# Layer 2 of a three-part fp32 kernel: the activation behind the next unit's copy, seven units' activation in the second product, some sums on VectorE

## The chip, the cores and the metric

One core of one Trainium2 chip runs the whole kernel. The metric is device time in microseconds (us) of one execution; all engines work from their own instruction queues and wait for each other through semaphores. The engines are named as in the profile: PE (TensorE matmul), PEld (its weight load), DVE (VectorE), ACT (ScalarE), POOL (GpSimd) and SP (the queue that issues the DMAs).

## The reference

Windowed attention, then a first MLP, then a second one. Only the second MLP is touched:

```python
x = attention(q, k, v)                      # 4 x 8 heads x 576 x 64, window 64, then (2304, 512)
x = leaky(x @ w_in, 0.01) @ w_out           # 512 -> 2048 -> 512
h = x @ w_in2                               # (2304, 2048)
g = np.maximum(h, 0.0) + np.log1p(np.exp(-np.abs(h)))
out = g @ w_out2                            # (2304, 512)
```

## The kernel before

All products are fp32. Each fp32 operand is held as a high and a low part (`split`: a cast on ACT, then a subtract on DVE or POOL), and one fp32 product is three matmuls (`three`). In the second MLP ("layer 2") the products are also blocked 2 x 2 by a seven-product scheme: the operands get sums of their quarters (`winograd`), seven products are made (`ORDER`), and `combine` puts them together.

**First product of layer 2.** It is 24 units. A unit n is a pair p of blocks of the hidden dimension (eight pairs) times a chunk c of 768 tokens (three chunks), listed in `order`. `products(n, p, c)` makes it: seven products of six matmuls 128x384, each in a PSUM bank of its own. The eight banks go round, so a product can start only when the bank of the product eight places earlier has been read: the third product of a unit (index 2) waits for `u2` of the unit before, for example. `combine` reads the banks: first a copy q1 on ACT (L707), then eight adds on DVE (L706) that write the tile h in two halves; the tiles `h_xh` and `h_xl` take turns. Then for each half: DVE sets the sign bit of a copy, which makes -|h| (L698, an integer OR), ACT makes softplus of it (L699) and the relu of h (L700), POOL adds the two (L701), and SP stores the sum into DRAM at `hd[p]` (L702). The copies of -|h| lie in five places that the program calls `act_places` (two in `cv`, three in `kept64`; from unit 17 on only three).

**Second product of layer 2.** It is 40 steps (`steps2`): four chunks of 512 tokens and one of 256, times eight pairs. A step is 42 matmuls 128x256 (L792, L799, L800). What the steps need is made ahead by `advance(i)`: the four sums of step i+3 (`sums`, L255 on DVE), the splits of step i+2 (`spread`, three casts L759 on ACT, three subtracts L760 on DVE), and the load of step i+5 from `hd` into one of four tiles `in` (`load_h`). After the eighth step of a chunk `put_out` combines the banks (eight adds 128x512 on DVE).

**Order of the work.** The order on each engine is that of the program text, moved by `later` and `ordered`, which merge the queues of one unit or step with those beside it. `todo[n]` lists what is put beside unit n: the splits of the input chunk c=2 (`split_x2`, units 1 and 2), the loads of weights (`load_first`, `load_second`) and their splits (`split_pair`, L236 cast on ACT and L237 subtract), and from unit 17 on the preparation of the second product's first three steps (`advance(-3)` to `advance(-1)`). Weights of the second product are split with POOL's subtracts, those of the first with DVE's.

Of the kernel before, what the change touches and what calls it, by code (L numbers as in the profile page):

```python
# [14 lines left out]
AF = mybir.ActivationFunctionType  # L15
ALU = mybir.AluOpType
# [4 lines left out]
def tile_window_attention_two_mlps(  # L21
# [138 lines left out]
    cv = sb.tile([P, 3, DM], F32, tag="cv", bufs=1, name="cv")  # L160
# [31 lines left out]
    def take_rows(i, p, rows):  # L192
        W["pair", i, p] = {o: (row[:, 0], row[:, 1]) for row, o in zip(rows, USED)}

    def load_row(i, p, row, o):
        if split_too(i, p):
            nc.sync.dma_start(row.bitcast(F32), wd[i][p][:, o].rearrange("p a h x -> p a (h x)"))
        else:
            nc.sync.dma_start(row[:, 1].bitcast(F32), wd[i][p][:, o].rearrange("p h x -> p (h x)"))

    pair_tiles = {}

# [7 lines left out]

    def split_pair(i, p):
        for t in pair_tiles.pop((i, p)):
            split(t[:, :, 0], t[:, :, 1], t[:, :, 1].bitcast(F32), nc.gpsimd if i == 1 else None)

    def load_first(p):
        tags = ENDS if p == NF // 2 - 1 else ODD if p % 2 else EVEN
# [18 lines left out]
    def split(hi, lo, a, eng=None):  # L235
        i = nc.scalar.copy(hi, a)  # L236
        j = (eng or nc.vector).tensor_tensor(lo, a, hi.bitcast(F32), ALU.subtract)  # L237
        return i.ins, j.ins

    def winograd(t, b, plus, eng=None):  # L240

        if plus:
            todo = (
                (0, b[1][0], b[1][1], ALU.add), (2, b[0][0], b[1][0], ALU.subtract),
                (1, t[0], b[0][0], ALU.subtract), (3, b[0][1], t[1], ALU.subtract),
            )
        else:
            todo = (  # L250
                (0, b[0][1], b[0][0], ALU.subtract), (2, b[1][1], b[0][1], ALU.subtract),
                (1, b[1][1], t[0], ALU.subtract), (3, b[1][0], t[1], ALU.subtract),
            )
        for n, x, y, op in todo:
            (eng or nc.vector).tensor_tensor(t[n], x, y, op)  # L255

    kept = {}
# [292 lines left out]
    def x_tile(tag, name, shape, dt):  # L550
        return sb.tile(shape, dt, tag=tag, bufs=2, name=name)
# [20 lines left out]
    def split_x2(c, kk):  # L572
        x, ts = stage["x"], stage["t"]
        b = [[x[:, i, h * TH : (h + 1) * TH] for h in range(2)] for i in range(2)]
        if kk == 0:
            XB[c] = [
                wide(f"xb_{c}_{n}").rearrange("p a b -> p (a b)").rearrange("p (h k x) -> p h k x", h=2, k=2)
                for n in range(7)
            ]
        winograd([ts[:, n] for n in range(4)], b, False, nc.gpsimd)  # L580
        for d, a in zip(XB[c], (b[0][0], b[1][0], b[1][1])):
            split(d[:, 0, kk], d[:, 1, kk], a)

# [89 lines left out]
    def products(n, p, c):  # L673

        if "h" not in stage:
            stage["h"] = turns([x_tile(nm, f"h_{nm}", [P, 2, 2 * TH], F32) for nm in ("xh", "xl")])
        w, x = W["pair", 0, p], XB[c]

        def product(a, b):
            ps = next_bank([P, TH], f"p_{n}_{a}")
            (wh, wl) = (t.rearrange("p (k f) -> p k f", k=2) for t in w[a])
            for kk in range(2):
                three(ps, wh[:, kk], wl[:, kk], x[b][:, 0, kk], x[b][:, 1, kk], kk == 0, kk == 1)
            return ps

        t = lambda nm: sb.tile([P, TH], F32, tag="tmp", bufs=4, name=f"{nm}_{n}")
        h = next(stage["h"])
        behind.append(  # L690
            combine(
                (product(*o) for o in ORDER), t("q1"), t("u2"), t("u3"), t("v"),
                ((h[:, 0, :TH], h[:, 0, TH:]), (h[:, 1, :TH], h[:, 1, TH:])),
            )
        )
        for a in range(2):
            g = next(act_places)
            nc.vector.tensor_scalar(g.bitcast(I32), h[:, a].bitcast(I32), -(2**31), None, ALU.bitwise_or)  # L698
            nc.scalar.activation(g, g, AF.Softplus)  # L699
            nc.scalar.activation(h[:, a], h[:, a], AF.Relu)  # L700
            nc.gpsimd.tensor_tensor(g, h[:, a], g, ALU.add)  # L701
            nc.sync.dma_start(hd[p][:, a, c * 2 * TH : (c + 1) * 2 * TH], g)  # L702

    def combine(made, q1, u2, u3, v, to):

# [16 lines left out]
    sets, A, HT, ready = {}, {}, {}, {}  # L722
# [5 lines left out]
    HS = 4  # L728
# [26 lines left out]
    def spread(i):  # L755
# [7 lines left out]
        for x in range(4):  # L763
            A[i][4 + x] = [t[:, x] for t in four]

    def advance(i):

        for f, n in ((sums, 3), (spread, 2), (load_h, 5)):
            if (HS if f is load_h else 0) <= i + n < len(steps2):
                f(i + n)  # L770

# [215 lines left out]
    for item in HEAD:  # L987
        n = len(item.rstrip("0123456789"))
# [76 lines left out]
    N = len(order)  # L1065
# [4 lines left out]
    for p in range(2, NPR):  # L1070
        n = last_of[p - 2] if p < NPR - 1 else 8
        todo[n] += [(load_first, p)]
        todo[n + 2] += [(split_pair, 0, p)]

    def act_place():
        two = [kept["cv"][:, n * 2 * TH : (n + 1) * 2 * TH] for n in range(2)]
        more = [t.bitcast(F32)[:, : 2 * TH] for t in kept["64"]]
        for n in range(2 * (N - 7)):
            yield (two + more)[n % 5]
        while True:  # L1080
            yield from two + more[:1]

    act_places = act_place()
    chunks = [(t0, min(TO, NT - t0)) for t0 in range(0, NT, TO)]
    steps2 = [(k, t0, n, p) for k, (t0, n) in enumerate(chunks) for p in range(NPR)]

# [94 lines left out]
```

## Time and profile before

| | |
|---|---|
| median of three runs | 882.7 us (881.86 to 886.53) |
| the profiled execution, its own time | 881.52 us |
| its span, first to last instruction | 879.7 us |
| mean granted clock of TensorE | 0.992 |
| busy: PE, DVE, ACT, POOL | 844.1 (96%), 615.3 (70%), 462.2 (53%), 257.4 us (29%) |
| first matmul of layer 2, of its second product, end of the last | 492.7, 691.0, 875.6 us |

Times of single rows are of the profiled execution. Busy times of PE are of overlapping matmuls, so a full PE shows no gap but its matmuls start one "pitch" apart.

### The profile page before, as it was taken

What the parts mean: (1) busy time and instruction counts of PE and PEld (TensorE: products, weight loads), DVE (VectorE), ACT (ScalarE), POOL (GpSimd) and SP (SyncE); (2) the same over time, 40 slices, a digit from 0 to 9 for tenths busy, and PEclk for the clock granted to TensorE, in tenths of its full rate; (3) what the DMA queues carried; (4) which work ended last, traced back from release to release, by engine and by line L of the source; (5) the groups of instructions that cost most, each with busy time, mean ns of one, the idle gap of its engine ahead of it and who ended that gap; (6) DMA issues with size and microseconds to landing.
All of it is one profiled execution on the core that took longest, in us unless ns stands there. A gap on an engine that the chain in (4) does not pass through costs nothing. (4 is left out here: it accounts for less than half of the span.)

```text
span 879.7 us, 16530 instructions
## 1 busy us (share of the span) xinstructions
PE 844.1 (96%) x6072; PEld 822.1 (93%) x6072; DVE 615.3 (70%) x1104; ACT 462.2 (53%) x1037; POOL 257.4 (29%) x287
## 2 busy tenths in 40 slices
PE   7799999999999999999999999999987899999998
PEld 5789999899999999999999989988987899999998
DVE  5899743535436654344668788887899899887965
ACT  5888643545445444545556456635555453343432
POOL 3211000103423333233345365534556840000000
PEclk9999999999999999999999999999998999999999
DMA  9787667455958876565855345434455596443412
GB/s 206 195 218 228 189 150 134 110 113 148 249 149 235 221 208 181 157 174 165 251 171 159 105 144 174 150 120 143 162 193 173 186 327 213 121 144 98 144 53 92
DMA packets 213714, 148.56 MB, mean 169 GB/s; under 512 B 104832, under 2 KB 184064, under 8 KB 213632
## 3 DMA queue, kind: packets, MB, share of 16 engines
q1 hardware_dynamic: 213632, 147.49, 58.3%
q8 instruction: 48, 0.79, 0.4%
q14 instruction: 34, 0.28, 0.1%
HBM read 99.22 MB, written 54.53 MB: 175 GB/s over the span
## 5 line engine op out<-in xcount | busy, mean ns | idle before, releaser
L625 DVE TENSOR_TENSOR gl<-g,gh 128x384 fp32r<-128x384 f32 x96 | 59.9, 624 | 130.6 <-ACT gh L619 108.0
L593 PE MATMUL o<-gh,w 128*128 128x384 f32 x384 | 130.8, 341 | 0.4 <-DVE x L659 0.2
L593 PE MATMUL ph<-xh,w 128*128 128x384 f32 x384 | 130.5, 340 | 0.0
L594 PE MATMUL o<-gl,w 128*128 128x384 f32 x384 | 128.6, 335 | 0.6 <-DVE gl L625 0.5
L595 PE MATMUL ph<-xh,w 128*128 128x384 f32 x384 | 128.4, 334 | 0.0
L594 PE MATMUL ph<-xl,w 128*128 128x384 f32 x384 | 128.4, 334 | 0.0
L595 PE MATMUL o<-gh,w 128*128 128x384 f32 x360 | 120.6, 335 | 0.0
L613 ACT ACTIVATE g<-ph 128x384 f32<-128x384 f32 x96 | 46.9, 488 | 117.2 <-PE ph L595 117.0
L593 PEld LDWEIGHTS o<-gh,w 128*128 128x128 f32 x384 | 72.1, 188 | 3.0 <-issue 1.2
L593 PEld LDWEIGHTS ph<-xh,w 128*128 128x128 f32 x384 | 72.1, 188 | 1.2 <-issue 0.5
L594 PEld LDWEIGHTS o<-gl,w 128*128 128x128 f32 x384 | 72.1, 188 | 1.1 <-DVE gl L625 1.1
L594 PEld LDWEIGHTS ph<-xl,w 128*128 128x128 f32 x384 | 72.2, 188 | 0.0
L595 PEld LDWEIGHTS ph<-xh,w 128*128 128x128 f32 x384 | 72.1, 188 | 0.0
L792 PE MATMUL f<-wq,a 128*128 128x256 f32 x252 | 71.4, 283 | 0.0
L799 PE MATMUL f<-wq,a 128*128 128x256 f32 x252 | 71.3, 283 | 0.0
L800 PE MATMUL f<-wq,a 128*128 128x256 f32 x252 | 71.3, 283 | 0.0
L497 ACT ACTIVATE sm<-sm,nm 128x128 f32<-128x128 f32 x144 | 55.9, 391 | 26.2 <-DVE nm L486 26.1
L595 PEld LDWEIGHTS o<-gh,w 128*128 128x128 f32 x360 | 67.6, 188 | 0.3 <-issue 0.3
L510 POOL TENSOR_TENSOR sm<-sm,sums 128x512 f32<-128x512 f32 x36 | 38.6, 1072 | 87.7 <-DVE sums L506 54.3
L759 ACT CAST a<-in 128x512 fp32r<-128x512 f32 (+1 forms) x40 | 23.0, 576 | 56.7 <-issue 46.8
L760 DVE TENSOR_TENSOR a<-kept,a 128x1024 fp32r<-128x1024 f32 (+1 forms) x40 | 47.9, 1197 | 6.7 <-ACT a L759 6.7
L619 ACT CAST gh<-g 128x384 fp32r<-128x384 f32 x96 | 49.3, 514 | 2.4
(303 smaller groups left out, 2329.6 us busy)
## 6 DMA issues: line engine op xcount, KB each, us to landing
in<-hd SPq DMA_DIRECT2D x32, 512.0 KB, 4.6
hd<-cv SPq DMA_DIRECT2D x24, 384.0 KB, 2.6
hd<-kept SPq DMA_DIRECT2D x24, 384.0 KB, 2.5
wraw<-in_moe_w_out_dram SPq DMA_DIRECT2D x16, 512.0 KB, 4.5
wraw<-in_moe_w_in_dram SPq DMA_DIRECT2D x16, 512.0 KB, 4.1
kept<-in_moe_w_in_dram SPq DMA_DIRECT2D x16, 512.0 KB, 4.6
kept<-in_moe_w_out_dram SPq DMA_DIRECT2D x16, 512.0 KB, 4.0
wd<-kept_part SPq DMA_DIRECT2D x11, 512.0 KB, 4.3
```

The lines of the kernel that those rows point to most:

```text
L497: nc.scalar.activation(sm[:, p, :], sm[:, p, :], AF.Exp, bias=nm[:, p : p + 1], accum_out=sums[:, p : p + 1],)
L510: nc.gpsimd.tensor_tensor(sm, sm, sums.unsqueeze(2).to_broadcast([P, NP, P]), ALU.mult)
L593: nc.tensor.matmul(ps, wh, xh, start=start, stop=False)
L594: nc.tensor.matmul(ps, wh, xl, start=False, stop=False)
L595: nc.tensor.matmul(ps, wl, xh, start=False, stop=stop)
L613: nc.scalar.activation(g, ph, AF.Prelu, alpha=0.01)
L619: a = nc.scalar.copy(gh, g)
L625: b = nc.vector.tensor_tensor(gl, g, gh.bitcast(F32), ALU.subtract)
L760: last = [nc.vector.tensor_tensor(lo, a, hi.bitcast(F32), ALU.subtract) for (hi, lo), a in parts][-1].ins
L792: j = nc.tensor.matmul(ps, gh, wh, start=first and u == 0, stop=False, skip_group_check=True)
L799: nc.tensor.matmul(ps, gh, wl, start=False, stop=False, skip_group_check=True)
L800: j = nc.tensor.matmul(ps, gl, wh, start=False, stop=end, skip_group_check=True)
```

## The change

1. Unit n's softplus, relu, POOL add and store are put into a list and issued behind unit n+1's first copy q1 (`later(activate, lag=1)`); the OR stays with unit n.
2. For seven pairs (pair, chunk) in `RAW`, units 1, 17, 18, 20, 21, 22 and 23, no activation is made in the first product: h is stored as it is by one DMA (for the three of chunk 2 only its first 512 of 768 tokens; the last 256 go the old way, both halves in shapes 128x512). The second product makes it: `awake(i)`, called by `advance` four steps ahead, does OR on DVE, softplus on ACT, and max and add in one DVE instruction, in place in the tile `in`. That is ten of the 40 steps (6, 12, 13, 14, 20, 21, 22, 29, 30, 31), of which 12 and 13 for half of the tokens.
3. The pairs of the first product are made in the order `PAIRS` (the second product keeps its order).
4. `split_pair` of the second product's weights: pairs 0 to 2 subtract on DVE, not on POOL.
5. The sums of the input chunk c=2 (`winograd`, eight adds 128x384 in units 1 and 2) run on DVE, not on POOL.

```diff
+    PAIRS = (4, 3, 0, 1, 2, 5, 6, 7)
     def load_row(i, p, row, o):
+        d = wd[i][p if i else PAIRS[p]]
...
     def split_pair(i, p):
         for t in pair_tiles.pop((i, p)):
-            split(t[:, :, 0], t[:, :, 1], t[:, :, 1].bitcast(F32), nc.gpsimd if i == 1 else None)
+            split(t[:, :, 0], t[:, :, 1], t[:, :, 1].bitcast(F32), nc.gpsimd if i == 1 and p > 2 else None)
...
-        winograd([ts[:, n] for n in range(4)], b, False, nc.gpsimd)
+        winograd([ts[:, n] for n in range(4)], b, False, None if c == 2 else nc.gpsimd)
...
-        for a in range(2):
-            g = next(act_places)
-            nc.vector.tensor_scalar(g.bitcast(I32), h[:, a].bitcast(I32), -(2**31), None, ALU.bitwise_or)
+        later(activate, lag=1)
+        unit, n, pair = n, 2 * TH, PAIRS[p]
+        m = min(NT // TO * TO - c * n, n) if (pair, c) in RAW else 0
+        if m:
+            nc.sync.dma_start(hd[pair][:, :, c * n : c * n + m], h[:, :, :m])
+        parts = [h] if m else [h[:, a : a + 1] for a in range(2)]
+        for i, x in enumerate(parts if m < n else ()):
...
+            nc.vector.tensor_scalar(g.bitcast(I32), x.bitcast(I32), -(2**31), None, ALU.bitwise_or)
+            acts.append((x, g, hd[pair][:, i : i + x.shape[1], c * n + m : (c + 1) * n]))
+
+    RAW = {(4, 1), (6, 0), (5, 1), (6, 1), (5, 2), (6, 2), (7, 2)}
+    acts = []
+
+    def activate():
+        while acts:
+            h, g, to = acts.pop(0)
             nc.scalar.activation(g, g, AF.Softplus)
-            nc.scalar.activation(h[:, a], h[:, a], AF.Relu)
-            nc.gpsimd.tensor_tensor(g, h[:, a], g, ALU.add)
-            nc.sync.dma_start(hd[p][:, a, c * 2 * TH : (c + 1) * 2 * TH], g)
+            nc.scalar.activation(h, h, AF.Relu)
+            nc.gpsimd.tensor_tensor(g, h, g, ALU.add)
+            nc.sync.dma_start(to, g)
...
+    def awake(i):
+        k, t0, n, p = steps2[i]
+        parts = [(max(t0, c * 2 * TH) - t0, min(t0 + n, (c + 1) * 2 * TH) - t0) for c in range(NX) if (p, c) in RAW]
+        parts = [x for x in parts if x[0] < x[1]]
+        if parts and n == TO:
+            h = HT["in"][i % HS][:, :2, parts[0][0] : parts[-1][1]]
+            g = kept["64"][0].bitcast(F32)[:, : 2 * h.shape[2]].rearrange("p (a x) -> p a x", a=2)
+            nc.vector.tensor_scalar(g.bitcast(I32), h.bitcast(I32), -(2**31), None, ALU.bitwise_or)
+            nc.scalar.activation(g, g, AF.Softplus)
+            nc.vector.scalar_tensor_tensor(h, h, 0.0, g, ALU.max, ALU.add)
+
     def advance(i):
-        for f, n in ((sums, 3), (spread, 2), (load_h, 5)):
+        for f, n in ((sums, 3), (spread, 2), (awake, 4), (load_h, 5)):
```

The places shift where the order moves. First ACT, between the first copies of unit 7 and unit 8 (`q1_7`, `q1_8`; `h_xh` is unit 6's tile there, `h_xl` unit 7's; `kept64` and `cv` are places of -|h|). Before:

```order
L707 COPY q1_7_6239<-p_7_0_6243 128x384
L699 ACTIVATE kept64_0_1587<-kept64_0_1587 128x768
L700 ACTIVATE h_xh_5650<-h_xh_5650 128x768
L699 ACTIVATE kept64_1_1588<-kept64_1_1588 128x768
L700 ACTIVATE h_xh_5650<-h_xh_5650 128x768
L699 ACTIVATE kept64_2_1589<-kept64_2_1589 128x768
L700 ACTIVATE h_xl_5651<-h_xl_5651 128x768
L699 ACTIVATE cv_104<-cv_104 128x768
L700 ACTIVATE h_xl_5651<-h_xl_5651 128x768
L707 COPY q1_8_6318<-p_8_0_6322 128x384
```

and with the change:

```order
L728 COPY q1_7_6222<-p_7_0_6226 128x384
L720 ACTIVATE cv_104<-cv_104 128x768
L721 ACTIVATE h_xh_5650<-h_xh_5650 128x768
L720 ACTIVATE cv_104<-cv_104 128x768
L721 ACTIVATE h_xh_5650<-h_xh_5650 128x768
L728 COPY q1_8_6301<-p_8_0_6305 128x384
L720 ACTIVATE kept64_0_1587<-kept64_0_1587 128x768
L721 ACTIVATE h_xl_5651<-h_xl_5651 128x768
L720 ACTIVATE kept64_1_1588<-kept64_1_1588 128x768
L721 ACTIVATE h_xl_5651<-h_xl_5651 128x768
```

Unit 7's four activations (on `h_xl`) stood ahead of `q1_8` and now stand behind it; ahead of it are only the four of unit 6.

Second, DVE from unit 18's last adds to unit 19's first, where the second product's first steps are prepared as well (L255/L258 sums, L760/L781 splits, L240 the subtract that POOL did before). Before:

```order
L706 TENSOR_TENSOR h_xh_5650<-p_18_2_7177,q1_18_7140 128x384
L706 TENSOR_TENSOR h_xh_5650<-p_18_7_7185,v_18_7143 128x384
L698 TENSOR_SCALAR kept64_0_1587<-h_xh_5650 128x768
L706 TENSOR_TENSOR h_xh_5650<-p_18_3_7193,u3_18_7142 128x384
L255 TENSOR_TENSOR kept64_2_1589<-in_1_7120 128x256
L698 TENSOR_SCALAR cv_104<-h_xh_5650 128x768
L255 TENSOR_TENSOR kept64_2_1589<-in_1_7120 128x256
L255 TENSOR_TENSOR kept64_2_1589<-kept64_2_1589,in_1_7120 128x256
L760 TENSOR_TENSOR a0_gl_7128<-in_0_7119,a0_gh_7127 128x256
L255 TENSOR_TENSOR kept64_2_1589<-in_1_7120,kept64_2_1589 128x256
L706 TENSOR_TENSOR u2_19_7212<-p_19_5_7223,q1_19_7211 128x384
```

and with the change:

```order
L727 TENSOR_TENSOR h_xh_5650<-p_18_7_7167,v_18_7125 128x384
L727 TENSOR_TENSOR h_xh_5650<-p_18_3_7175,u3_18_7124 128x384
L258 TENSOR_TENSOR kept64_2_1589<-in_1_7102 128x256 x2
L240 TENSOR_TENSOR wq0_5_7113<-wq0_5_7113 128x3x256
L240 TENSOR_TENSOR wq1_2_7114<-wq1_2_7114 128x2x256
L727 TENSOR_TENSOR u2_19_7185<-p_19_5_7196,q1_19_7184 128x384
L258 TENSOR_TENSOR kept64_2_1589<-kept64_2_1589,in_1_7102 128x256
L727 TENSOR_TENSOR u3_19_7186<-p_19_6_7204,u2_19_7185 128x384
```

Unit 18's two ORs (L698) are gone, since it is stored raw, and two subtracts of weights have come in ahead of `u2_19`.

Third, DVE in the second product, where step 6 is awakened (L794, L796 on the tile `in_2`), behind the splits of step 4 and ahead of the sums of step 6. Before:

```order
L760 TENSOR_TENSOR a1_1_7368<-kept64_1_1588,a1_0_7367 128x1024
L255 TENSOR_TENSOR kept64_1_1588<-in_2_7121 128x256 x2
L255 TENSOR_TENSOR kept64_1_1588<-kept64_1_1588,in_2_7121 128x256
L255 TENSOR_TENSOR kept64_1_1588<-in_2_7121,kept64_1_1588 128x256
L760 TENSOR_TENSOR a2_1_7372<-in_1_7120,a2_0_7371 128x512
L760 TENSOR_TENSOR a2_gl_7374<-in_1_7120,a2_gh_7373 128x256
L760 TENSOR_TENSOR a2_1_7372<-kept64_2_1589,a2_0_7371 128x1024
```

and with the change:

```order
L781 TENSOR_TENSOR a1_1_7332<-kept64_1_1588,a1_0_7331 128x1024
L794 TENSOR_SCALAR kept64_0_1587<-in_2_7103 128x1024
L796 SCALAR_TENSOR_TENSOR in_2_7103<-in_2_7103,kept64_0_1587 128x1024
L258 TENSOR_TENSOR kept64_1_1588<-in_2_7103 128x256 x2
L258 TENSOR_TENSOR kept64_1_1588<-kept64_1_1588,in_2_7103 128x256
L258 TENSOR_TENSOR kept64_1_1588<-in_2_7103,kept64_1_1588 128x256
L781 TENSOR_TENSOR a2_1_7336<-in_1_7102,a2_0_7335 128x512
L781 TENSOR_TENSOR a2_gl_7338<-in_1_7102,a2_gh_7337 128x256
L781 TENSOR_TENSOR a2_1_7336<-kept64_2_1589,a2_0_7335 128x1024
```

The two rows L794 and L796 are new; between them stands one softplus on ACT, of the same tile, for which L796 waits.

## Rows read from the trace of the kernel before

**Rows 1.** Windows: stretch, length, busy of PE, PEld, DVE, ACT, POOL, PEclk, DMA, GB/s.
```profile
492.70:632.80 140.10, 133.60 (x759) 130.68 (x758) 116.06 (x198) 77.40 (x131) 71.22 (x41) 1.00 0.43 146
603.60:618.10 14.50, 14.50 (x85) 14.50 (x84) 10.58 (x21) 8.96 (x16) 8.76 (x5) 1.00 0.53 173
632.80:691.00 58.20, 49.28 (x254) 47.42 (x253) 55.19 (x78) 29.65 (x48) 37.13 (x23) 0.91 0.59 192
640.00:700.00 60.00, 48.82 (x265) 46.74 (x264) 59.57 (x82) 30.85 (x49) 38.97 (x23) 0.91 0.55 178
691.00:729.30 38.30, 35.98 (x295) 35.56 (x296) 35.68 (x53) 22.18 (x37) 20.48 (x14) 1.00 0.80 281
729.30:850.20 120.90, 120.90 (x1010) 120.90 (x1009) 101.75 (x195) 48.04 (x76) 0.00 (x0) 1.00 0.41 126
```

**Rows 2.** Waits of PE, 490 to 625 us: total, times, longest.
```profile
PE p L593 <- DVE u L706: 3.5, 4, 2.5
PE p L593 <- ACT q L707: 1.7, 2, 1.1
PE p L593 <- DVE h_xh L706: 1.3, 1, 1.3
```

**Rows 3.** Waits of PE, 625 to 720 us.
```profile
PE p L593 <- DVE u L706: 4.1, 3, 2.0
PE p L593 <- DVE h_xl L706: 3.9, 1, 3.9
PE f L792 <- DVE h_xl L706: 2.3, 1, 2.3
```

**Rows 4.** Timeline around the first copy of unit 8 (start, us).
```profile
559.23 0.85 ACT L699 ACTIVATE kept<-kept 128x768 f32<-128x768 f32 x1 [2.71 <-DVE kept L698]
...
559.70 0.56 DVE L698 TENSOR_SCALAR cv<-h_xl 128x768 int32<-128x768 int32 x1
...
562.19 0.46 ACT L707 COPY q<-p 128x384 f32<-128x384 f32 x1
...
562.68 0.56 DVE L706 TENSOR_TENSOR u<-p,q 128x384 f32<-128x384 f32 x1 [2.42 <-ACT q L707]
```

**Rows 5.** DVE by line and shape, 640 to 700 us: busy, mean ns, idle.
```profile
L255 DVE TENSOR_TENSOR kept<-in 128x256 f32<-128x256 f32 x10 | 10.1, 1030 | 1.8 <-DMA hd<-kept 1.8
L760 DVE TENSOR_TENSOR a<-kept,a 128x1024 fp32r<-128x1024 f32 x3 | 6.4, 2141 | 0.0
L255 DVE TENSOR_TENSOR kept<-kept,in 128x256 f32<-128x256 f32 x5 | 5.3, 1068 | 0.0
L255 DVE TENSOR_TENSOR kept<-in,kept 128x256 f32<-128x256 f32 x5 | 5.1, 1018 | 0.0
L760 DVE TENSOR_TENSOR a<-in,a 128x512 fp32r<-128x512 f32 x3 | 3.7, 1231 | 0.0
L760 DVE TENSOR_TENSOR a_gl<-in,a_gh 128x256 fp32r<-128x256 f32 x3 | 3.5, 1166 | 0.0
```

**Rows 6.** DVE by line and shape, 720 to 850 us.
```profile
L760 DVE TENSOR_TENSOR a<-kept,a 128x1024 fp32r<-128x1024 f32 x26 | 31.8, 1222 | 6.3 <-ACT a L759 6.3
L255 DVE TENSOR_TENSOR kept<-in 128x256 f32<-128x256 f32 x48 | 18.2, 421 | 1.1 <-DMA in<-hd 0.4
L760 DVE TENSOR_TENSOR a<-in,a 128x512 fp32r<-128x512 f32 x26 | 17.9, 687 | 0.9 <-ACT a L759 0.6
L760 DVE TENSOR_TENSOR a_gl<-in,a_gh 128x256 fp32r<-128x256 f32 x26 | 11.0, 422 | 6.1 <-ACT a_gh L759 6.1
```

**Rows 7.** POOL by line and shape, 632.8 to 704 us.
```profile
L701 POOL TENSOR_TENSOR cv<-h_xl,cv 128x768 f32<-128x768 f32 x5 | 10.4, 2094 | 8.7 <-ACT h_xl L700 8.7
```

**Rows 8.** Timeline of the second product, steps 18 and 19 being prepared.
```profile
779.05 1.22 DVE L760 TENSOR_TENSOR a<-kept,a 128x1024 fp32r<-128x1024 f32 x1
...
782.71 1.22 DVE L760 TENSOR_TENSOR a<-kept,a 128x1024 fp32r<-128x1024 f32 x1
...
784.71 0.28 PE L792 MATMUL f<-wp_v,a 128*128 128x256 f32 x1
```

**Rows 9.** Timeline of ACT, a weight load that is waited for.
```profile
642.62 0.83 ACT L236 CAST wq<-wq 128x768 fp32r<-128x768 f32 x1 [1.64 <-DMA wq<-wd]
```

More of the change, by code (lines that the diff above doesn't have):

```diff
@@ L193, in take_rows @@
         W["pair", i, p] = {o: (row[:, 0], row[:, 1]) for row, o in zip(rows, USED)}
+    PAIRS = (4, 3, 0, 1, 2, 5, 6, 7)
     def load_row(i, p, row, o):
+        d = wd[i][p if i else PAIRS[p]]
         if split_too(i, p):
-            nc.sync.dma_start(row.bitcast(F32), wd[i][p][:, o].rearrange("p a h x -> p a (h x)"))
+            nc.sync.dma_start(row.bitcast(F32), d[:, o].rearrange("p a h x -> p a (h x)"))
         else:
-            nc.sync.dma_start(row[:, 1].bitcast(F32), wd[i][p][:, o].rearrange("p h x -> p (h x)"))
+            nc.sync.dma_start(row[:, 1].bitcast(F32), d[:, o].rearrange("p h x -> p (h x)"))
     pair_tiles = {}
@@ L695, in products @@
         )
-        for a in range(2):
-            g = next(act_places)
-            nc.vector.tensor_scalar(g.bitcast(I32), h[:, a].bitcast(I32), -(2**31), None, ALU.bitwise_or)
+        later(activate, lag=1)
[5 more added lines that the diff above has]
+        for i, x in enumerate(parts if m < n else ()):
+            x = x[:, :, m:]
+            pool = act_places[: 3 if unit >= N - 7 else 5]
+            pool.sort(key=lambda t: t[0])
+            pool[0][0] += 5
+            g = pool[0][1][:, : x.shape[1] * (n - m)].rearrange("p (a x) -> p a x", a=x.shape[1])
+            nc.vector.tensor_scalar(g.bitcast(I32), x.bitcast(I32), -(2**31), None, ALU.bitwise_or)
[5 more added lines that the diff above has]
+            h, g, to = acts.pop(0)
             nc.scalar.activation(g, g, AF.Softplus)
-            nc.scalar.activation(h[:, a], h[:, a], AF.Relu)
-            nc.gpsimd.tensor_tensor(g, h[:, a], g, ALU.add)
-            nc.sync.dma_start(hd[p][:, a, c * 2 * TH : (c + 1) * 2 * TH], g)
+            nc.scalar.activation(h, h, AF.Relu)
+            nc.gpsimd.tensor_tensor(g, h, g, ALU.add)
+            nc.sync.dma_start(to, g)
     def combine(made, q1, u2, u3, v, to):
@@ L1073, in tile_window_attention_two_mlps @@
         todo[n + 2] += [(split_pair, 0, p)]
[L1075 to L1083, printed above, removed]
+    act_places = [kept["cv"][:, n * 2 * TH : (n + 1) * 2 * TH] for n in range(2)]
+    act_places += [t.bitcast(F32)[:, : 2 * TH] for t in kept["64"]]
+    act_places = [list(x) for x in enumerate(act_places)]
     chunks = [(t0, min(TO, NT - t0)) for t0 in range(0, NT, TO)]
@@ L1134, in tile_window_attention_two_mlps @@
             later(f, *a)
+    activate()
     queues = {}
```

## The prediction

> **What bounds the kernel now.** The busy time by stretch comes first, since PE does all the products. One stretch without any stop, two units of the first product, gives 84 matmuls in some 14.55 us [rows 1]: 7.28 us a unit. The stretch of units 0 to 17 lasts 140.1 us; at this pace it would last 18 x 7.28 = 131.0. PE loses 9.1 us there. Units 18 to 23 last 58.2 us and would last 43.7: 14.5 us lost. The first steps of the second product lose 38.3 - 36.0 = 2.3. From 729.3 to 850.2 us PE is busy in all of 120.9 us, 0.12 us a matmul and 5.03 us a step [rows 1]: nothing is lost there, and nothing that is put on another engine can gain there. So layer 2 has 25.9 us to give, and all of it lies ahead of 693 us.
>
> The waits of PE say who is late. Up to unit 17 it is the combine: 3.5 and 1.3 us for DVE's adds and 1.7 for the copy q1, 6.5 in all [rows 2]; from 625 us on it is DVE alone, 10.3 us [rows 3]. Why DVE is late differs in the two.
>
> In units 0 to 17 the timeline shows a chain of two engines. Unit 7's second OR ends at 560.3 us and ACT begins its four activations at 559.2; only at 562.19 does it come to unit 8's first copy, and DVE, which needs the copy, stood idle for 2.42 us before its next add at 562.68 [rows 4]. Copy (0.46), eight adds, OR, four activations (2.96 from 559.23 to 562.19), next copy: each waits for the one before, round and round, so the loop takes as long as a unit of PE, and whatever stretches a link is never caught up. DVE has the time: it is busy for 116.1 of the 140.1 us [rows 1].
>
> From 640 to 700 us DVE has none: busy for 59.6 of 60 us [rows 1]. Part of that is stretched time. A sum of 128x256 takes 1.03 us there and 0.42 after 720 us, where POOL is still; the subtract of 128x1024 takes 2.14 and 1.22 [rows 5, 6]. Over the 29 instructions of these shapes the excess is (10.1 - 4.2) + (5.3 - 2.1) + (5.1 - 2.1) + (6.4 - 3.7) + (3.7 - 2.1) + (3.5 - 1.3) = 18.6 us. POOL is busy for 39.0 us of that minute [rows 1], so a microsecond of POOL costs DVE 0.48. The granted clock falls as well, to 0.91, in the stretch where PE stops; in the others it is 1.00 [rows 1], and part of the 14.5 us is this: 254 matmuls show 49.3 us of busy time where 254 x 0.173 is 44.0.
>
> **The late activation (part 1 of the change).** Nothing is added on any engine; softplus, relu, POOL's add and the store come behind the next unit's q1. The copy then waits for four activations of two units ago at most, which had a whole unit of time, and no longer for the adds of its own predecessor. The loop is cut, and the 1.7 us on the copy and the DVE idle time behind it go. What is late instead is POOL's add and the store, by a unit; behind the store on SP's queue stand the weight loads of the units ahead, which have two units until their split, so about 7 us remain for a load. DVE's own peaks remain, such as the weight splits beside a busy POOL. I keep 1.5 of the 9.1 us: -7.6. Bounds: all 9.1 goes, or only the 1.7 on the copy and half of the rest, -5.4.
>
> **The sums of c=2 on DVE (part 5).** Eight adds of 384 columns: at 0.42 us for 256 [rows 6] at most 0.63 each, 5.0 us in units 1 and 2. DVE has 24 us of idle time in the stretch [rows 1] and loses the stretching by POOL's eight. I take nothing; without that cover 5.0. **The order of the pairs (part 3)** moves names and loads, not amounts: nothing, at worst the wait for one late load, 1.6 us [rows 9].
>
> **Raw units, and splits on DVE (parts 2 and 4), units 18 to 23.** POOL loses the adds of 18 and 20 wholly, of 21 to 23 two thirds, and the splits of three pairs. What stays: unit 19's two adds at 2.09 [rows 7] and three thirds, 2 x 2.09 + 3 x 1.4 = 8.4 us of 39.0. At 0.48 the stretching falls from 18.6 to 4.0 us: 14.6 saved on DVE. The ORs of 18 and 20 go and two thirds of three more: four at 0.56 [rows 4] and as much again, about 4.2. Three pairs of weights come: 1792 columns each, at 1.22 us per 1024 [rows 6] 2.1 us, 6.4 in all. DVE's 59.6 us become 59.6 - 14.6 - 4.2 + 6.4 = 47.2. PE's own work of that minute is at most its busy 48.8 [rows 1]. So DVE falls to PE's pace, hardly below it: most of the loss goes, and with it the clock's, but DVE has nothing in hand against a late copy or load. Of 14.5 + 2.3 = 16.8 I keep 2.5: -14.3. Bounds: 0 kept, or 8 (half).
>
> The Trainium skill, page "SBUF — State Buffer", section "Who interferes with whom", calls the port that DVE and GpSimd share an exclusive lock: whoever comes first blocks the other for its whole instruction, and a DVE operation with two SBUF inputs needs it. This fits stretching by a half to the whole of POOL's time, and it would let the 8.4 us that stay cost up to 8.4, not 4.0.
>
> **Awakening (part 2, second product).** Per full step: an OR of 1024 columns, 0.56 x 1024/768 = 0.75 [rows 4]; softplus on ACT, 0.85 x 1024/768 = 1.13 [rows 4], for which DVE waits, as the next instruction on its queue is the max-add; behind that stand the sums of the step after, and PE's operands behind them. The max-add has no row. The nearest is the two-input subtract of 128x1024, 1.22 us alone and 2.14 beside POOL [rows 5, 6]; POOL is still after 729 us, so I take 1.22. With hand-offs some 3.2 us, between 2.9 and 4.1. A step costs DVE 3.66 us now (779.05 to 782.71) against PE's 5.03: 1.37 to spare a step. And DVE is ahead: step 18's splits end at 780.27, PE wants them at 784.71, 4.4 us later [rows 8], and this is just after a chunk's combine, when the lead is least. Steps 20, 21, 22 are awakened one behind the other from there: 4.4 - 3 x (3.2 - 1.37) = -1.1 us. Steps 12 to 14 include two of half size, 29 to 31 begin a step later, step 6 stands alone: they end above zero. So +1.0, between 0 and 4.4 - 3 x (4.1 - 1.37) = -3.8. Of ten awakenings, some 29 us of DVE and ACT time, the lead hides all but this.
>
> **Sum.** Made against the profiled execution's 881.5 us (span 879.7 and 1.8 around it), which stands 1.2 below the median of 882.7: 881.5 - 7.6 - 14.3 + 1.0 = 860.6 us.
>
> **Rivals.**
> - *Late loads take DVE's place* (before 691 us). A cast of weights waited 1.64 us for its DMA [rows 9]; now a DVE subtract stands behind such casts and ahead of `u2_19` and its like, so a late load stops the combine, where POOL used to take the wait. Three pairs at 1.6 to 3 us, on a DVE without slack: 865 to 870. Against it: raw stores wait neither for ACT nor for POOL, so the loads behind them on SP start earlier.
> - *POOL's remaining adds block DVE for their whole time.* 8.4 instead of 4.0 us, on the path: 865. For it: forms with less work (128x256) are stretched by 0.6 us each, out of proportion to their size [rows 5, 6].
> - *DVE falls behind in the second product.* If an awakening takes 4.1 us, or the softplus waits behind ACT's casts, the steps 20 to 22 lose 3.8, the other two threes 1 to 2 each: 6 us more, 866. For it: DVE already waits for ACT's casts there [rows 6].
> - *The other side: the lead is not there.* If ACT, not DVE, sets the preparation, the ten awakenings lie bare: 8 x 3.2 + 2 x 1.9 = 29.4, and 860.6 - 1.0 + 29.4 = 889. It decides, that is the kernel is slower, from 2.7 us of PE wait per awakening (26 us against the 21.9 gained and the half per cent). Against it: PE has no wait at all after 729 us [rows 1], and ACT is busy for 48 of 120.9.
> - *POOL is not what stretches DVE.* Then 640 to 700 us keeps 18.6 us of stretching, and the moved subtracts come stretched, some 12 us: 881.5 - 7.6 + 5 = 879, no change. Against it: the shapes' times fall just where POOL stops [rows 1, 5, 6].
>
> **Chances.** The forecast, 855 to 864.5, has 0.60; late loads 0.15; POOL's remaining adds 0.08; awakening late 0.09; the lead not there 0.04; POOL not the cause 0.04. The range from 855 to 870 holds the first four but for their edges, some 0.83. Half a per cent, 4.4 us, is about what a measurement of this kernel can tell from no change: faster than 878 has 0.91, between 0.05, slower than 887 has 0.04.
>
> **What would show it.** Right: units 0 to 17 in 131 to 134 us, the copy q1 without its predecessor's activations ahead of it; 640 to 690 us with DVE's sums at 0.4 to 0.6 us and the clock at 1.00; the second product starting near 670 us; in the second product a PE wait of 0 to 4 us near steps 20 to 23 and none elsewhere. Wrong: PE waits for DVE behind a subtract of weights (the loads); sums still at 1 us (POOL is not the cause); gaps on PE at each awakened step (no lead).

## The result and the profile after

The changed kernel takes 859.14 us (median of four runs, 857.62 to 859.99), the kernel before 884.31 beside it; the ratio is 0.9714, 95% interval 0.9679 to 0.9749: faster by 2.9%. The profiled execution took 858.35 us, with a span of 856.5. Forecast were 860.6.

The windows of the changed kernel, with columns as in [rows 1]: units 0 to 17, units 18 to 23, the first eight steps of the second product, and its other full steps.

```profile
493.80:626.00 132.20, 131.34 (x758) 131.02 (x757) 115.43 (x210) 76.29 (x130) 59.60 (x32) 1.00 0.48 163
626.00:669.70 43.70, 43.70 (x254) 43.70 (x253) 41.11 (x79) 20.06 (x34) 6.97 (x5) 1.00 0.75 242
669.70:710.00 40.30, 40.30 (x338) 40.30 (x337) 37.74 (x61) 19.38 (x35) 12.67 (x11) 1.00 0.81 271
710.00:831.20 121.20, 121.20 (x1011) 121.08 (x1010) 109.81 (x207) 54.00 (x86) 0.00 (x0) 1.00 0.39 120
```

PE is busy in all of the last three, at a clock of 1.00; the 58.2 us of units 18 to 23 in [rows 1] are 43.7 now, which is 6 x 7.28. Of the 6.5 and 10.3 us of waits of [rows 2, 3], the second of which has the second product's start in it, the waits of PE from 490 us to the end leave two:

```profile
PE p L597 <- DVE xb L240: 0.9, 1, 0.9
PE f L832 <- DVE a L781: 0.2, 1, 0.2
```

PE loses more than it is shown to wait, as its matmuls also start further apart around a wait. Measured from first matmul to first matmul, all units take 7.28 us but unit 3, which takes 8.45; all full steps take 5.04 but step 30, which takes 0.2 more; and step 36, one of the half-size steps at the end, takes 0.6 more than its neighbours. That last loss follows a late load:

```profile
834.30 3.78 SPq L758 DMA_DIRECT2D in<-hd  x3
...
840.13 0.49 DVE L258 TENSOR_TENSOR kept<-in 128x128 f32<-128x128 f32 x2 [2.08 <-DMA in<-hd]
...
842.35 0.38 PE L832 MATMUL f<-wp_sm,a 128*128 128x256 f32 x1 [0.19 <-DVE a L781]
```

SP issues these loads at 834.30, behind the stores of a combine's result; DVE stands idle for 2.08 us for one of them, and PE then waits for DVE.

The timeline at unit 8's first copy answers to [rows 4]:

```profile
553.24 0.33 PE L596 MATMUL p<-xb,wp_raw 128*128 128x384 f32 x1
...
554.52 0.48 ACT L728 COPY q<-p 128x384 f32<-128x384 f32 x1 [2.52 <-issue]
...
555.65 0.55 DVE L727 TENSOR_TENSOR u<-p,q 128x384 f32<-128x384 f32 x1
```

The copy comes at 554.52, 1.3 us after the unit's first matmul, as soon as its six are done; ACT waited for them. Before, it came at 562.19, 7.8 us after its unit's first matmul and behind four activations of unit 7.

### The profile page after: what moved, and what is told of

Read it like the earlier page. It is cut to its first block, busy times and chain, and to the rows that moved or that the text cites. A ratio compares the mean times of both kernels' runs of the same rounds, so it can differ in the third digit from the quotient of the medians.

```text
span 856.5 us, 16466 instructions
## 1 busy us (share of the span) xinstructions
PE 836.2 (98%) x6072; PEld 818.4 (96%) x6072; DVE 608.5 (71%) x1132; ACT 452.3 (53%) x1025; POOL 207.9 (24%) x257
## 4 chain that ended last, share of the span: by engine, by line
PE 86%; DVE 5%; DMA 3%; ACT 3%; issue 1%; SPq 1%; POOL 0%; DVEq 0%; ACTq 0%
PE o L596 7%; PE ph L596 7%; PE o L598 7%; PE o L597 7%; PE ph L598 7%; PE ph L597 7%; PE f L832 7%; PE f L824 7%; PE f L831 7%; PE p L597 6%; PE p L598 6%; PE p L596 6%; PE po L910 2%; PE pt L522 1%; PE ps L880 1%
## 5 line engine op out<-in xcount | busy, mean ns | idle before, releaser
L513 POOL TENSOR_TENSOR sm<-sm,sums 128x512 f32<-128x512 f32 x36 | 38.5, 1071 | 88.0 <-DVE sums L509 49.2
L622 ACT CAST gh<-g 128x384 fp32r<-128x384 f32 x96 | 49.2, 512 | 2.5
L832 PEld LDWEIGHTS f<-wq,a 128*128 128x128 f32 x252 | 48.4, 192 | 0.1
L831 PEld LDWEIGHTS f<-wq,a 128*128 128x128 f32 x252 | 48.4, 192 | 0.0
```

The lines of the kernel that those rows point to most:

```text
L513: nc.gpsimd.tensor_tensor(sm, sm, sums.unsqueeze(2).to_broadcast([P, NP, P]), ALU.mult)
L622: a = nc.scalar.copy(gh, g)
L831: nc.tensor.matmul(ps, gh, wl, start=False, stop=False, skip_group_check=True)
L832: j = nc.tensor.matmul(ps, gl, wh, start=False, stop=end, skip_group_check=True)
```

## The experiments

A length that each trace gives is that of layer 2, from its first matmul to the end of the span. It leaves out what differs ahead of it: the first matmul of layer 2 stands between 492.7 and 498.3 us in these traces, though hardly a part of the change lies ahead of it. Two traces of the changed kernel agree in layer 2 to 0.1 us. Each length below is of one trace, and lengths of units and steps are from first matmul to first matmul.

Each ratio is to runs of the kernel before on the same chip (medians 884.0 to 885.5 us there).

| kernel | median, us | ratio to before, 95% interval | first matmul of layer 2 | layer 2, us |
|---|---|---|---|---|
| before | 882.7 | | 492.7 | 387.0 |
| changed | 859.14 | 0.9714 (0.9679 to 0.9749) | 493.8 | 362.7 |
| changed, again | 858.92 | 0.9701 (0.9678 to 0.9724) | 493.5 | 362.7 |
| late activation alone | 871.80 | 0.9862 (0.9819 to 0.9904) | 498.3 | 376.3 |
| raw units alone | 872.12 | 0.9848 (0.9820 to 0.9877) | 495.8 | 375.1 |
| subtracts on DVE alone | 885.03 | 0.9992 (0.9975 to 1.0008) | 497.3 | 386.8 |
| all but the late activation | 866.99 | 0.9805 (0.9780 to 0.9830) | 493.9 | 370.2 |
| all but the raw units | 871.18 | 0.9853 (0.9819 to 0.9886) | 496.1 | 374.0 |
| all but the subtracts on DVE | 862.72 | 0.9755 (0.9725 to 0.9784) | 493.5 | 365.0 |
| all but the sums on DVE | 860.03 | 0.9722 (0.9695 to 0.9749) | 496.9 | 361.7 |
| all but the order of pairs | 858.99 | 0.9718 (0.9691 to 0.9745) | 495.4 | 361.9 |
| all but these two | 857.55 | 0.9683 (0.9660 to 0.9706) | 494.1 | 362.2 |
| changed, POOL kept busy | 868.82 | 0.9832 (0.9802 to 0.9861) | 493.6 | 371.5 |
| changed, two awakenings more | 864.91 | 0.9784 (0.9763 to 0.9806) | 493.7 | 368.7 |

Every kernel of the table but the first and "subtracts on DVE alone" also picks the place for -|h| as the changed one does, the one used longest ago; no run takes this apart.

**The late activation alone.** Parts 2 to 5 are taken back (of the four edits, that of part 2):

```diff
-    RAW = {(4, 1), (6, 0), (5, 1), (6, 1), (5, 2), (6, 2), (7, 2)}
+    RAW = set()
```

> The kernel before with the late activation alone (softplus, relu, POOL add and store of unit n behind unit n+1's first copy; no raw units, sums and splits on POOL as before). Theory A (the ring copy, adds, OR, activations, next copy costs units 3 to 17 their 7 to 9 us; from unit 18 on it is DVE's own load): units 0 to 17 in 131 to 134 us, units 18 to 23 as slow as before; 872 to 877 us, ratio 0.988 to 0.993. Theory B (the raw units and the work taken off POOL are what frees the first product; the place of the activations alone does little): 880 to 884 us.

871.8 us, and 10.7 us less in layer 2: theory A's mechanism, with a median and a ratio just below its range. Its windows, units 0 to 17, then 18 to 23:

```profile
498.27:631.25 132.98, 131.72 (x758) 130.92 (x757) 122.89 (x205) 79.15 (x134) 74.81 (x42) 1.00 0.47 159
631.25:684.44 53.19, 47.23 (x254) 44.95 (x254) 51.33 (x72) 28.32 (x44) 37.43 (x22) 0.97 0.61 194
```

In the first 18 units PE idles 1.3 us instead of 6.5, all of it at unit 3. From unit 18 on the cause is as before, DVE busy for 51.3 of 53.2 us, POOL for 37.4, and PE idle for 6.0; but these units are not "as slow as before": they took 58.2 us [rows 1], at a clock of 0.91. So 5.0 of the gain lie here, 7.1 in units 0 to 17, and the second product gives 1.4 back.

**All but the late activation.**

```diff
-        later(activate, lag=1)
...
             acts.append((x, g, hd[pair][:, i : i + x.shape[1], c * n + m : (c + 1) * n]))
+        activate()
```

> The changed kernel with the activations back at their own unit, ahead of the next unit's first copy; everything else changed. Theory A: units 3 to 17 lose 6 to 9 us again, units 18 to 23 hardly any, since most of them have no activation left: 865 to 869 us. Theory B (freed POOL and DVE are enough): 859 to 861 us.

867.0 us, 7.5 us longer in layer 2, in theory A's range, but not where it put it:

```profile
493.90:628.79 134.89, 132.23 (x757) 130.87 (x757) 112.52 (x204) 74.76 (x127) 57.54 (x31) 1.00 0.45 152
628.79:675.50 46.71, 43.98 (x254) 43.65 (x253) 42.72 (x82) 19.89 (x36) 8.80 (x6) 1.00 0.72 235
```

In units 0 to 17 PE idles 2.7 us, not 6 to 9, and 0.9 of that is at unit 3, as in the changed kernel; in units 18 to 23 it idles another 2.7, in one wait for `u2` at unit 21. The other 1.8 us are in the second product. Unit by unit, the ring holds 7.28 us in most units and loses at two: unit 10 takes 7.9 us and unit 13 takes 9.3. They took 10.1 and 9.5 in the kernel before, and take 10.1 and 9.3 with raw units alone; in every kernel with the late activation both take 7.28. So the ring is no steady loss; it has nothing in hand at some units. Why at these two is not shown. The late activation is also what gives DVE its lead behind unit 18.

**All but the raw units.**

```diff
-    RAW = {(4, 1), (6, 0), (5, 1), (6, 1), (5, 2), (6, 2), (7, 2)}
+    RAW = set()
```

> The changed kernel without raw units: every unit's activation in the first product, no awakening in the second; the late activation and the sums and splits on DVE stay. Theory A (POOL's adds stretch DVE between 640 and 700 us, at 0.48 us per us of POOL): POOL keeps some 32 of its 39 us there, DVE has 6.4 us of splits more than before, so units 18 to 23 and the start of the second product lose 12 to 18 us: 871 to 877 us. Theory B (the late activation frees units 18 to 23 too, the awakenings only cost): 858 to 862 us.

871.2 us, 11.3 us longer in layer 2: theory A's time, but not all where it put it. Units 18 to 23 lose 2.5 us and steps 0 and 3 of the second product 6.6, 9.1 together and not 12 to 18; 3.3 us more than in the changed kernel are lost at unit 3. Waits of PE from 640 us:

```profile
PE f L824 <- DVE u L727: 2.0, 2, 1.5
PE p L596 <- DVE h_xl L727: 1.9, 1, 1.9
PE f L832 <- DVE a L781: 1.8, 2, 1.6
```

All are for DVE. Another wait of 2.6 us stands at unit 3, for the split of its operands, where the changed kernel waits 0.9. That unit 1's activation makes DVE and ACT come to it later is likely, and not shown apart.

**All but the subtracts on DVE.**

```diff
-            split(t[:, :, 0], t[:, :, 1], t[:, :, 1].bitcast(F32), nc.gpsimd if i == 1 and p > 2 else None)
+            split(t[:, :, 0], t[:, :, 1], t[:, :, 1].bitcast(F32), nc.gpsimd if i == 1 else None)
```

> The changed kernel with the second product's weight subtracts of pairs 0 to 2 back on POOL. Theory A (by the rows, 0.48 us of DVE per us of POOL): DVE loses 6.4 us of work and gains some 3.2 of stretching; DVE is not late anyway: 858 to 860 us, no change. Theory B (an exclusive port, all of POOL's time on DVE): 6.7 us of stretching against 6.4 of work, the same balance, but POOL's adds and subtracts come late behind each other: PE waits for weights or sums at the start of the second product, 861 to 866 us.

862.7 us and 2.3 us longer in layer 2: theory A's "no change" falls, and theory B's mechanism too, for PE does not wait at the start of the second product. It waits for `a`, 1.1 us in four waits: two at step 21 and one at step 30, both awakened, and one at step 36. DVE comes later to the combine ahead of them, and the rows of the two kernels show it, first this one's, then the changed kernel's (DVE's first add, and PE's first matmul of step 16):

```profile
749.60 1.48 DVE L727 TENSOR_TENSOR in<-f,in 128x512 f32<-128x512 f32 x2
...
750.18 0.28 PE L824 MATMUL f<-wp_at,a 128*128 128x256 f32 x1
```
```profile
747.97 2.08 DVE L727 TENSOR_TENSOR in<-f,in 128x512 f32<-128x512 f32 x3
...
750.34 0.28 PE L824 MATMUL f<-wp_at,a 128*128 128x256 f32 x1
```

0.6 us ahead of PE against 2.4. What DVE loses at 640 to 700 us it still lacks 50 us and more later. Both theories had POOL's part too small. These subtracts take POOL about twice what they take DVE, as three of them show, first here, then in the changed kernel:

```profile
L240 POOL TENSOR_TENSOR wq<-wq 128x768 fp32r<-128x768 f32 x3 | 5.7, 1898 | 13.9 <-ACT wq L239 13.9
```
```profile
L240 DVE TENSOR_TENSOR wq<-wq 128x768 fp32r<-128x768 f32 x3 | 2.9, 952 | 0.7 <-ACT wq L239 0.7
```

From 626 to 710 us POOL is busy for 34.4 us here and for 19.6 in the changed kernel: 14.7 us of subtracts, not 6.7. At 0.48 they stretch DVE by 7.1 us, not 3.2, which is about the work that DVE is spared. Why DVE comes later all the same is not shown.

**The subtracts on DVE alone**, in the kernel before:

```diff
-            split(t[:, :, 0], t[:, :, 1], t[:, :, 1].bitcast(F32), nc.gpsimd if i == 1 else None)
+            split(t[:, :, 0], t[:, :, 1], t[:, :, 1].bitcast(F32), nc.gpsimd if i == 1 and p > 2 else None)
```

> The kernel before with the second product's weight subtracts of pairs 0 to 2 on DVE and nothing else. Theory A (by the rows: DVE full between 640 and 700 us, 6.4 us of work more and 3.2 us of stretching less): 3 us slower, 885 to 888 us, with DVE at 59 us and more of 60 in that stretch. Theory B (an exclusive port: POOL's 6.7 us less are 6.7 us of DVE more): no difference, 882 to 885 us. Theory C (the subtracts come late on POOL, behind its adds, and what they hold up matters more than DVE's work): faster, 878 to 881 us.

0.9992: no difference, theory B's number, and theory A's 3 us lie outside the interval. But the number does not speak for B's mechanism. With the 14.7 us that the subtracts take on POOL, theory A's own price gives 7.1 us less of stretching against 6.4 of work, which is no difference, and theory B's would take some 8 us more off DVE than it gets. By these estimates the run fits the price of about a half. PE's loss only moved: units 18 to 23 take 53.4 us instead of 58.2, the second product 192.8 instead of 188.8, with waits of 3.7 us for `a` in its first steps.

**POOL kept busy**, with work whose result nobody uses:

```diff
+        if unit in (18, 20, 21, 22, 23):
+            d = kept["64"][0].bitcast(F32)[:, 2 * TH : 2 * TH + 2 * P]
+            for _ in range(6):
+                nc.gpsimd.tensor_tensor(d, h[:, 0, : 2 * P], h[:, 1, : 2 * P], ALU.add)
```

> The changed kernel with work for POOL that nobody waits for: beside units 18, 20, 21, 22 and 23 six adds 128x256 of two halves of h each into an unused part of a place (the outputs are as before). That gives POOL back some 25 us in the 44 us before the second product. DVE has 2.6 us idle there. Theory A (POOL's time stretches DVE, 0.3 to 0.5 us per us): DVE gets 8 to 12 us longer, its sums stand at 0.8 to 1.0 us again, and PE loses 5 to 10 us: 864 to 870 us. Theory B (DVE was late for its own amount of work, not for POOL): 858 to 861 us. By the rule of an exclusive port up to the whole 25 us: 875 us or more.

868.8 us, 8.8 us longer in layer 2, in theory A's range. Its windows:

```profile
626.00:669.70 43.70, 43.70 (x255) 43.70 (x254) 42.09 (x73) 17.96 (x31) 23.75 (x22) 1.00 0.65 211
669.70:710.00 40.30, 34.94 (x268) 33.71 (x268) 36.47 (x50) 18.29 (x33) 25.41 (x24) 0.96 0.79 266
```

POOL is busy for 49.2 us of these 84 where it was for 19.6. Now DVE's two-input forms in the 84 us, in the changed kernel and then here (columns as in [rows 5]):

```profile
L781 DVE TENSOR_TENSOR a<-kept,a 128x1024 fp32r<-128x1024 f32 x10 | 12.7, 1272 | 0.3 <-ACT a L780 0.3
L258 DVE TENSOR_TENSOR kept<-in 128x256 f32<-128x256 f32 x22 | 12.6, 605 | 0.2
L781 DVE TENSOR_TENSOR a<-in,a 128x512 fp32r<-128x512 f32 x10 | 8.1, 806 | 0.6 <-ACT a L780 0.6
L258 DVE TENSOR_TENSOR kept<-in,kept 128x256 f32<-128x256 f32 x11 | 5.7, 516 | 0.2
L258 DVE TENSOR_TENSOR kept<-kept,in 128x256 f32<-128x256 f32 x11 | 5.1, 464 | 0.0
L781 DVE TENSOR_TENSOR a_gl<-in,a_gh 128x256 fp32r<-128x256 f32 x10 | 4.7, 469 | 0.0
```
```profile
L258 DVE TENSOR_TENSOR kept<-in 128x256 f32<-128x256 f32 x19 | 12.9, 707 | 0.2
L785 DVE TENSOR_TENSOR a<-kept,a 128x1024 fp32r<-128x1024 f32 x8 | 11.4, 1420 | 0.0
L785 DVE TENSOR_TENSOR a<-in,a 128x512 fp32r<-128x512 f32 x8 | 7.6, 955 | 0.0
L258 DVE TENSOR_TENSOR kept<-kept,in 128x256 f32<-128x256 f32 x9 | 6.7, 740 | 0.0
L785 DVE TENSOR_TENSOR a_gl<-in,a_gh 128x256 fp32r<-128x256 f32 x8 | 5.3, 669 | 0.0
L258 DVE TENSOR_TENSOR kept<-in,kept 128x256 f32<-128x256 f32 x9 | 4.8, 531 | 0.2
```

Against the undisturbed means of [rows 6] the excess is 7.7 us in the changed kernel and 15.0 here: 0.39 and 0.31 us per microsecond of POOL, where [rows 1, 5, 6] gave 0.48; the run with the subtracts back on POOL gives 0.44 by the same sum (15.2 of 34.4). So that POOL's work stretches DVE is shown, with fewer instructions here (61 against 74) that lose more.

That stretching makes the 8.8 us is shown only in part. All of them are lost in the second product; PE idles 5.4 us in the window of the first steps, where the clock is 0.96, and steps 0, 4 and 5 take 2.4, 1.7 and 4.3 us longer than 5.04. What stands ahead of two of them is not a stretched DVE:

```profile
688.26 0.52 SPq L727 DMA_DIRECT2D hd<-cv  x1
...
690.02 0.57 SPq L762 DMA_DIRECT2D in<-hd  x1
...
694.41 0.39 PE L835 MATMUL f<-wp_sm,a 128*128 128x256 f32 x1 [1.42 <-POOL wp_sm L240]
...
695.46 0.83 DVE L798 TENSOR_SCALAR kept<-in 128x1024 int32<-128x1024 int32 x1 [2.37 <-DMA in<-hd]
...
700.89 0.39 PE L836 MATMUL f<-wq,a 128*128 128x256 f32 x1 [1.78 <-DVE a L785]
```

At step 4 PE waits 1.4 us for POOL itself, whose subtract stands behind the added work. Ahead of step 5, SP's queue waits 7.6 us for a sum of POOL that it has to store, the load behind that store leaves at 690.02 instead of 678.62, and DVE stands idle for it for 2.4 us. So of the three only step 0, where PE waits for the combine, is left for a DVE that is late by itself. What stretching alone costs PE here is not shown.

**Two awakenings more**, of steps 23 and 24, into the scratch place:

```diff
-        if parts and n == TO:
+        extra = i in (23, 24)
+        parts = parts or [(0, TO)] * extra
+        if parts and n == TO:
...
-            nc.vector.scalar_tensor_tensor(h, h, 0.0, g, ALU.max, ALU.add)
+            nc.vector.scalar_tensor_tensor(g if extra else h, h, 0.0, g, ALU.max, ALU.add)
```

> The changed kernel with two awakenings more, of steps 23 and 24, whose result goes into the scratch place (the outputs are as before), so that five steps in a row are awakened. An awakening takes 2.96 us of DVE in the trace of the changed kernel, 1.6 more than a step has to spare. Theory A (the lead hid the three, and is spent with them): PE waits at steps 22 to 25 and again near 30, 3 to 6 us more in all: 862 to 865 us. Theory B (DVE has time enough there, lead or not): 858 to 860 us. Theory C (an awakening stops PE wherever it stands): gaps of 2.5 to 3 us at every awakened step, those of the changed kernel too, which its trace does not show.

864.9 us, 6.0 us longer in layer 2: theory A, at its upper end. Waits of PE from 700 us:

```profile
PE f L826 <- DVE in L727: 2.1, 1, 2.1
PE f L834 <- DVE a L781: 1.4, 3, 0.5
PE f L826 <- DVE res_xl L727: 0.3, 1, 0.3
```

They stand at steps 22 to 24, none at the awakened steps ahead of them, which speaks against theory C; and the largest, 2.1 us, is for the combine, which DVE reaches late. Near step 30, where theory A had more of them, there is none.

**All but the sums on DVE; all but the order of pairs; all but these two.**

```diff
-        winograd([ts[:, n] for n in range(4)], b, False, None if c == 2 else nc.gpsimd)
+        winograd([ts[:, n] for n in range(4)], b, False, nc.gpsimd)
```

```diff
-    PAIRS = (4, 3, 0, 1, 2, 5, 6, 7)
+    PAIRS = (0, 1, 2, 3, 4, 5, 6, 7)
...
-    RAW = {(4, 1), (6, 0), (5, 1), (6, 1), (5, 2), (6, 2), (7, 2)}
+    RAW = {(0, 1), (6, 0), (5, 1), (6, 1), (5, 2), (6, 2), (7, 2)}
```

> The changed kernel with the sums of the input chunk c=2 back on POOL. Its trace shows one wait of PE in the first product, 0.9 us at unit 3 for DVE's split of these sums. Theory A (idle time of DVE hides the sums): no difference beyond 1 us, 858 to 860 us. Theory B (the sums on DVE make that wait): it goes, 857 to 858. Theory C (on POOL they come later, behind the late adds, and stretch DVE's splits): the wait at unit 3 grows to 2 to 5 us, 861 to 864 us.

> The changed kernel with the pairs in their old order; the second unit is still raw, so that the steps 8 and 16 are awakened, and 12 and 20 no longer. Theory A (the order moves names, not amounts; a run of two awakenings spends less lead than one of three): 857 to 860 us, with no PE wait at steps 20 to 23. Theory B (the order is needed, since step 8 is prepared while POOL still stretches DVE, or a load comes late): PE waits near steps 8 to 14, 861 to 864 us.

With the sums on POOL the wait at unit 3 is gone and layer 2 is 1.0 us shorter: theory B by the trace. With the old order PE's wait of 0.2 us in the second product is gone and layer 2 is 0.8 us shorter: theory A. The medians, 860.0 and 859.0 us, don't tell either from the changed kernel. So both were undone together, beside the changed kernel on the same chip:

> The changed kernel with the pairs in their old order and the sums of chunk c=2 on POOL, the two parts whose undoing took away a wait each (1.1 us at unit 3, some 0.4 us near the steps 30 and 31). Theory A (the two add up): layer 2 without a wait of PE, 1 to 2 us below the changed kernel, 856 to 859 us. Theory B (on POOL the sums shift POOL's adds, and the second product starts with less lead, as in the run with the sums on POOL alone): the gain at unit 3 is given back at steps 21 to 31, no difference.

> The changed kernel once more, as the partner on the same chip for the runs beside it. 857 to 861 us; PE waits 0.9 us at unit 3 and 0.2 us in the second product, as in its first trace.

857.55 against 858.92 us, layer 2 at 362.2 against 362.7; the changed kernel has its two waits again. The first product is without a loss (24 units in 174.7 us), but PE waits 0.7 us for the combine at step 16, so theory B has its part; the intervals overlap, and this version is not shown to be faster.

**Raw units alone**, with activations, sums, subtracts and order as before:

> The kernel before with seven raw units and ten awakenings alone: activations at their own unit, sums and weight subtracts on POOL, pairs in their old order. The late activation alone gave 12 us, the whole change 25. Theory A (two separate gains that add up): 12 to 14 us, 870 to 873 us; units 4 to 17 lose 5 to 8 us as before. Theory B (the parts overlap, since a raw unit 1 and a freed POOL also let the ring keep the lead that it has): units 4 to 17 lose 1 to 4 us, 862 to 869 us.

872.1 us, 11.9 us less in layer 2: theory A in time, and at the lower end of its loss, 5.0 us in units 4 to 17. Its windows, units 0 to 17 and 18 to 23:

```profile
495.78:631.80 136.02, 132.07 (x757) 130.89 (x757) 111.85 (x196) 74.33 (x127) 67.39 (x39) 1.00 0.45 150
631.80:679.19 47.39, 44.71 (x253) 43.47 (x253) 42.25 (x75) 17.75 (x33) 22.27 (x15) 1.00 0.67 221
```

PE idles for 4.0 us in the first and for 2.7 in the second, with POOL at 22.3 of 47.4 us. The late activation alone gave 10.7 and this 11.9; together with the rest 24.3. The two gains nearly add up. The rest has its part: without the late activation, parts 3 to 5 on top of the raw units bring layer 2 from 375.1 to 370.2 us.

## Why the prediction was right, step by step

The sum was 881.5 - 7.6 - 14.3 + 1.0 = 860.6; the profiled execution shows 881.5 - 24.3 in layer 2 and 1.1 of a later start, 858.3. By stretches the 24.3 are 7.9 in units 0 to 17, 14.5 in units 18 to 23 and 1.9 in the second product. The mechanisms were right; several sizes were not, and part of the agreement is luck, since errors of either sign met.

- **Units 0 to 17, -7.6.** 140.1 us became 132.2: -7.9. The mechanism is shown: the copy follows its product at once, and the late activation alone takes the idle time from 6.5 to 1.3 us. The size is right by two errors. The 1.5 us that the prediction kept back are not needed: where the sums of c=2 stay on POOL, units 0 to 17 take 131.04 us, and all of the 9.1 is gone. What is left, 1.2 us, is made by those sums. Nor is the late activation the only cure: the 3.4 us that were lost at units 3 to 7 go with raw units alone as well, while those at units 10 and 13 stay there.
- **The sums of c=2 on DVE, nothing.** Mis-sized: 1.2 us at unit 3, 1.0 of layer 2 (the trace with them on POOL). The cover named, DVE's idle time over 140 us, is an average; the split that unit 3 waits for has none of it.
- **The order of the pairs, nothing.** It moves names in the first product, as said, but also the awakened steps, and costs about 0.8 us of layer 2; no measured time shows it.
- **Units 18 to 23 and the start of the second product, -14.3.** 14.5 us became nothing, and so did the start, which step by step lost 3.0 us and not 2.3 (2.7 at step 0, 0.3 at step 4): -17.5. That DVE falls to PE's pace and hardly below it fits, as it is still busy for 41.1 of 43.7 us. The step that it would have "nothing in hand" was too careful by 3.2 us: the lead comes from the late activation, and without it PE waits 2.7 us at unit 21. POOL is what stretched DVE, as the run with a busy POOL shows, though not how much of PE's loss that was; the price of 0.48 us was somewhat high, the other three traces give 0.31, 0.39 and 0.44.
- **The rule of the Trainium skill**, page "SBUF — State Buffer", section "Who interferes with whom", is that the port of the two engines is an exclusive lock. That the two engines delay each other agrees with these runs; that all of POOL's time could fall on DVE was no trace's case: 29.5 us more of POOL cost DVE 7.3 us in the forms shown, a quarter.
- **Awakenings, 3.2 us each and +1.0.** The timeline of the changed kernel, at the awakening of step 21:

```profile
761.37 1.22 DVE L781 TENSOR_TENSOR a<-kept,a 128x1024 fp32r<-128x1024 f32 x1
...
762.51 0.69 DVE L794 TENSOR_SCALAR kept<-in 128x1024 int32<-128x1024 int32 x1
...
763.23 1.06 ACT L795 ACTIVATE kept<-kept 128x1024 f32<-128x1024 f32 x1 [3.79 <-DVE kept L794]
...
764.32 1.23 DVE L796 SCALAR_TENSOR_TENSOR in<-in,kept 128x1024 f32<-128x1024 f32 x1 [1.13 <-ACT kept L795]
...
767.99 1.22 DVE L781 TENSOR_TENSOR a<-kept,a 128x1024 fp32r<-128x1024 f32 x1
...
770.50 0.28 PE L824 MATMUL f<-wp_raw,a 128*128 128x256 f32 x1
```

From one large subtract to the next are 6.62 us; without an awakening it was 3.66 [rows 8]: 2.96 each. The max-add takes 1.23 us, the value that was taken from the nearest row, and 2.96 is at the lower end of the range of 2.9 to 4.1. Step 20's splits end at 769.21 and PE wants them at 770.50: 1.3 us in hand after two awakenings, where the prediction's arithmetic gives 4.4 - 2 x 1.83 = 0.7. So the three fit, just, and nothing of the +1.0 is lost at steps 20 to 23, where the prediction put it. PE loses at steps 30 and 36 instead, 0.2 and 0.6 us, behind the three awakenings of steps 29 to 31, which were to "end above zero". The run with two more shows where the lead ends. From 690.96 to the end of the span the kernel before took 188.8 us, 3.0 of them lost at steps 0 and 4; from 669.72 the changed one takes 186.8: the second product costs 1.1 us more by this, 0.8 of it at those two steps. That it is near the forecast 1.0 is luck. With the pairs in their old order, and as many awakenings, no step loses anything.

Of the rivals none came in the changed kernel with its price: PE does not wait behind a subtract of weights, and there is no gap at each awakened step. A late load does take DVE's place, but one of `in` and not of weights, and in the second product: it stands ahead of the 0.6 us at step 36. In the run with a busy POOL such a load held DVE for 2.4 us. Late weights were not tried.

## What to carry to other kernels

Look for a ring of two engines whose trip takes as long as the bound engine's unit: it may hold the pace in most units, but it has nothing in hand in the others; moving what nobody waits for behind the ring's first link gives it a lead. Work may be moved from a full stretch into one with slack, but the slack is a store that is filled and spent: count the lead where it is smallest, the run of moved pieces behind it, and what arrives late from the stretch ahead. An engine that nobody waits for still has a price if it stretches another, and that price is read from the same instruction with it busy and with it still. Before a longer time is put down to that price, look at each wait of the bound engine: work added to a queue also delays all that stands behind it, a store and the loads behind that store among them.

## What the runs showed of the hardware that was not expected

The part ahead of layer 2, attention and the first MLP, ends at times 5.6 us apart (492.7 to 498.3 us) from trace to trace, and the text of the program doesn't sort them: the kernel before and the same kernel with only later subtracts moved stand at 492.7 and 497.3. All of the difference arises in the first 145 us: from the 901st matmul, which starts between 139.1 and 144.6 us, to layer 2 every trace takes 353.6 or 353.7. Why is not shown. That is more than most parts of this change are worth, and why lengths within layer 2 were compared.
